# Four input tiles transposed by DMA on SyncE's queue instead of by TensorE, and the loads around them in a new order

## The chip, the cores and the metric

The kernel runs on one core of a Trainium2 chip. The metric is device time in microseconds. A core has TensorE (PE: matmuls and transposes into PSUM; PEld is its weight load, which runs beside it), VectorE (DVE), ScalarE (ACT), GpSimd (POOL) and SyncE (SP). SP, ACT and POOL each issue DMA transfers, which all share 16 DMA engines. Each engine executes its own instructions in order and waits on semaphores for the others.

## The reference

The input x has 2048 rows of 640 features. Rows are normalised; the result feeds a dilated sliding-window attention (32 heads of 20, window of 8 positions, 2 apart) and a gated product, and both are added to x.

```python
xn = _layernorm(x)                          # (2048, 640)
# attention
q, k, v = split(xn @ wqkv)                  # 32 heads of 20
idx = pos[:, None] - 2 * arange(8)          # 8 earlier positions, 2 apart
logits = einsum("bhsd,bhswd->bhsw", q, k[idx]) * Dh ** -0.5   # masked to -1e9 where idx < 0
o = einsum("bhsw,bhswd->bhsd", softmax(logits), v[idx])
A = o.reshape(B, S, D) @ wo
# gated product, 1536 wide
Bout = ((xn @ w_gate) * (xn @ w_up)) @ w_down
return x + A + Bout
```

All inputs, weights and the output are bfloat16.

## The kernel before

The 2048 rows are 16 tiles of 128 rows, and 4 chunks of 4 tiles. Nothing is issued as it is written in the source: every step is added to a plan (`add`) with an engine, a cost in us, what it depends on, and for transfers a size (`kb`) or a time before which they are not thought to land (`floor`). `Plan.order` then walks the engines like a list scheduler, each time taking the step with the least slack, and the program is emitted in that order. So costs, floors and dependences decide the order of instructions on every engine, in the whole kernel.

For each tile t, `ln(t)` makes the statistics on VectorE (`ln_stats` L251, twice; `ln_aggr` L257 and L259), GpSimd the reciprocal root (`ln_rstd` L265), VectorE again the normalised tile, in place (`ln_apply` L270). Tiles of x come from a pool of 5 buffers. `transposes(t)` then puts the tile, transposed, into `xnT` of its chunk (2 buffers):

- tiles 0 to 3: two groups of TensorE transposes (L345), each copied out of PSUM at L351;
- tiles 4 to 7 (t under `XDMA`, 8): five TensorE transposes of 128x128 (L331) into one PSUM tile, and one ScalarE copy (L335);
- tiles 8 to 15: one DMA transpose on SP's queue (L339).

At its end `transposes(t)` loads tile t+5 (L166): tiles 5 to 7 on SP, tiles 8 to 12 on ACT's queue, 13 to 15 on POOL's.

Per chunk, TensorE computes q and k (`qk`, L403, copied out by ScalarE at L410) and v (`vproj`, L436, copied out at L442 and stored to a scratch `vD` in device memory by POOL, L457). `prodlog` makes, for each of the 8 window positions, the elementwise product of q with the shifted k (VectorE, L474, 1.4 us each), and after four of them TensorE sums over the head's features into the logits (`lg`, L484, 20 matmuls). A few values are masked (L496, first chunk only), ScalarE copies the logits out (L497), and a DMA transpose on SP (L505, "LT") puts rows on partitions. `softmax` (L519 to L541) needs both LT transposes of the chunk. `load_v8(t)` reads the 8 shifted values of tile t back from `vD` (1280 KB, SP, L551, 3 buffers); `av` multiplies them with the weights and sums (L571, L580, L584, L586), and the result goes through a DMA transpose (L593, "oT").

`glu` is 12 pairs of matmul groups (L610) with wg and wu, copied out by ScalarE (L615) and multiplied on VectorE into hT (L626). `down` adds the products with wd (L648) and wo (L651) in one PSUM tile, VectorE adds x (L657), and the result is stored (L679). PSUM has 6 rotating banks ("ps") for all groups but the logits, which have two of their own ("pl").

Transfers on SP are issued in program order. The ones the change touches are, before: x0 to x3, wq, x4, wk, x5 to x7, wg, wu, the values of tile 0, wd, the first LT transpose, the values of tile 1, the second LT transpose, wo in four pieces (L231), the values of tile 2, the third LT transpose (chunk 1).

Of the kernel before, what the change touches and what calls it, by code (L numbers as in the profile page):

```python
# [9 lines left out]
ACT = mybir.ActivationFunctionType  # L10
# [21 lines left out]
class Plan:  # L32
# [8 lines left out]
    def add(self, eng, cost, fn, deps=(), occ=None, after=(), kb=0):  # L41
        s = Step(eng, cost, fn, deps, occ, after)
        s.kb = kb
        s.idx = len(self.steps)
        self.steps.append(s)
        return s
# [51 lines left out]
def kernel(  # L98
# [11 lines left out]
    nc = tc.nc  # L110
# [15 lines left out]
    CH = 4  # L126
# [36 lines left out]
    def load_x(t, eng=None):  # L163
        def fn():
            x = new(("x", t), [P, D], BF, "x", 5)
            (eng or nc.sync).dma_start(out=x[:], in_=x_flat[t * P : (t + 1) * P, :])  # L166
        return fn
# [3 lines left out]
    def wload(dst, src, eng=None):  # L171
        return lambda: (eng or nc.sync).dma_start(out=dst[:], in_=src.rearrange("(i p) f -> p i f", p=P))
# [9 lines left out]
    def load(at, fn, deps=()):  # L182
        s = chain[0] = add("SP", 2.0, fn, deps, occ=0.45, after=[chain[0]])
        s.floor = at
        return s
# [110 lines left out]
        XT[t] = inline("DVE", 0.443, ln_apply(t), [RS[t]], 0.4)  # L296

    def ln(t):
        turn = [XT.get(t - (2 if t < CH else 1)), GL.get(t - 1)] if t <= CH else []
        a = add("DVE", 0.48, ln_stats(t, 0), [X[t], GL.get(t - 3), *turn], occ=0.395)  # L300
        a = add("DVE", 0.48, ln_stats(t, 1), [a], occ=0.395)
        a = GL[t] = add("DVE", 0.39, ln_aggr(t), [a], occ=0.3)
        b = RS[t] = add("POOL", 0.56, ln_rstd(t), [a])
        XT[t] = add("DVE", 0.443, ln_apply(t), [b], occ=0.35)
# [10 lines left out]
        main = add("PE", cost + 0.165, fn, [main, *waits, *deps], occ=cost)  # L315
        return main

    XDMA = 8
    GP = {}

    def transposes(t):
        c, q = divmod(t, CH)

        def slot():
            if q == 0:
                new(("xnT", c), [P, KT, CS], BF, "xnT", 2)

        def pe():
            ps = new(("pst", t), [P, KT, P], BF, "ps", 6, psum)
            for g in range(KT):  # L330
                nc.tensor.transpose(ps[:, g, :], T["x", t][:, g * P : (g + 1) * P], ident[:])  # L331

        def ev():
            slot()
            nc.scalar.copy(T["xnT", c][:, :, q * P : (q + 1) * P], T["pst", t][:])  # L335

        def dma():
            slot()
            nc.sync.dma_start_transpose(out=T["xnT", c][:, :, q * P : (q + 1) * P], in_=T["x", t][:])  # L339

        def half(g0, g1, n):
            def pe():
                ps = new(("pst", t, n), [P, KT, P], BF, "ps", 6, psum)
                for g in range(g0, g1):
                    nc.tensor.transpose(ps[:, g, :], T["x", t][:, g * P : (g + 1) * P], ident[:])  # L345

            def ev():
                if n == 0:
                    slot()
                o, i = T["xnT", c][:, g0:g1, q * P : (q + 1) * P], T["pst", t, n][:, g0:g1, :]  # L350
                nc.scalar.copy(o, i) if t or n == 0 else nc.vector.tensor_copy(o, i)  # L351
            return pe, ev

        if t < CH:
            pa, ea = half(0, 3, 0)
            pb, eb = half(3, KT, 1)
            a = pe_main(0.17, pa, [XT.get((t, 0), XT[t])])
            TX[t] = add("ACT", 0.5, ea, [a], occ=0.42)
            ring.append(TX[t])
            a = pe_main(0.11, pb, [XT[t]])  # L360
            if t:
                TT[t] = add("ACT", 0.42, eb, [a, TX[t]], occ=0.33)
                behind(VE[t - 1][0], TT[t])
            else:
                TT[t] = inline("DVE", 0.4, eb, [a], 0.33)
            ring.append(TT[t])
        elif t < XDMA:
            a = pe_main(0.28, pe, [XT[t]])
            TT[t] = add("ACT", 0.695, ev, [a], occ=0.6)
            ring.append(TT[t])  # L370
        else:
            a = TT[t] = add("SP", 2.8, dma, [XT[t], GP.get(c - 2)], occ=1.28, kb=200)
        if t + 5 < W:
            X[t + 5] = load(11.9 + 0.45 * t, load_x(t + 5), [a])
        elif t + 5 < NT:
            e, dge = ("ACT", nc.scalar) if t < XDMA else ("POOL", nc.gpsimd)
            X[t + 5] = add(e, 6.0, load_x(t + 5, dge), [a], occ=0.45, kb=0 if t < XDMA else 160)

    Q, Kk, LASTPW = {}, {}, {}
    HALOCP = {}  # L380
# [85 lines left out]
    def prodlog(c):  # L466
        for g in range(2):
            n = 2 * c + g
            for j in range(4):
                i = 4 * g + j  # L470

                def mul(i=i):
                    p = new(("pw", c, i), [P, KT, CS], BF, "pw", 5)
                    nc.vector.tensor_tensor(p[:], T["q", c][:], T["k", c][:, :, DIL * i : DIL * i + CS], ALU.mult)  # L474

                m = 8 * c + i
                PW[m] = add("DVE", 1.48, mul, [*Q[c], *Kk[c], LL.get((m - 5) // 4) if m >= 5 else None], occ=1.395)
            LASTPW[c] = PW[m]

            def lg(g=g):  # L480
                l = new(("lps", c, g), [P, 512], F32, "pl", 2, psum)
                for i in range(KT):
                    for j in range(4):
                        nc.tensor.matmul(l[H * j : H * (j + 1), :], lhsT=Ek[:, i, :], rhs=T["pw", c, 4 * g + j][:, i, :],  # L484
                                         start=(i == 0), stop=(i == KT - 1), tile_position=(0, H * j),
                                         skip_group_check=True)

            LL[n] = add("PE", 1.28, lg, [*[PW[8 * c + 4 * g + j] for j in range(4)], LE.get(n - 2), CE], occ=1.195)
            LL[n].urgent = True
            LL[n].margin = 1.0  # L490

            def ev(g=g):
                L = new(("L", c, g), [P, CS], BF, "L", 2)
                if c == 0:
                    ps = T["lps", c, g]
                    nc.vector.tensor_tensor(ps[:, 0:HALO], ps[:, 0:HALO], negm[:, g, :], ALU.add)  # L496
                nc.scalar.copy(L[:], T["lps", c, g][:])  # L497

            LE[n] = add("ACT", 0.585, ev, [LL[n], SS.get(n - 2), CM], occ=0.5)

            def tr(g=g):
                if g == 0:
                    new(("LT", c), [P, CH, W, H], BF, "LT", 1)
                out = T["LT", c][:].rearrange("p t (g w) h -> p t g (w h)", g=2)[:, :, g, :]
                nc.sync.dma_start_transpose(out=out, in_=T["L", c, g][:])  # L505

            early = [SPLAST[0]] if c == 0 else []
            SS[n] = SPLAST[0] = add("SP", 3.5, tr, [LE[n], DD.get(2 * c - 1), DD.get(2 * c - 2)], occ=1.25, after=early, kb=160)
            if c == 0 and g == 0:
                load_v8(1)  # L510
                SPLAST[0] = V8[1]

    def softmax(c, hf):
        n = 2 * c + hf
# [30 lines left out]
    def load_v8(t):  # L545
        def fn():
            v = new(("v8", t), [P, W, D], BF, "v8", 3)
            r0 = t * P
            src = vD[r0 : r0 + P, :]
            src = bass.AP(tensor=src.tensor, offset=src.offset, ap=[[D, P], [DIL * D, W], [1, D]])  # L550
            nc.sync.dma_start(out=v[:], in_=src)  # L551
        order = [SPLAST[0]] if t < CH - 1 else [SS[2 * (t // CH) + 1]] if t % CH in (1, 2) else []
        V8[t] = add("SP", 6.0, fn, [VS[t], VS.get(t - 1), O16.get(t - 3), CZ], occ=0.5, after=order, kb=1280)
        if t < 3:
            SPLAST[0] = V8[t]
            V8[t].floor = (30.5, 0, 0)[t]

    def load_down():
        WL["d"] = SPLAST[0] = add("SP", 8, wload(wd, B_w_down), after=[SPLAST[0]], occ=0.5, kb=1920)

    def load_out():
        WL["o"] = SPLAST[0] = add("SP", 8, wo_load, after=[SPLAST[0]], occ=2.7, kb=1100)
# [154 lines left out]
    vproj(2, (1,))  # L717
    CE = add("POOL", 1.2, consts_e, [C0, RS[3]])
    CM = add("POOL", 1.1, consts_m, [CE])
    WL["g"] = load(17.2, wload(wg, B_w_gate))  # L720
    WL["u"] = load(23.2, wload(wu, B_w_up))
    qk(0, 0, CS, (0,))
    for t in (4, 5):
        ln(t)
        transposes(t)
    qk(0, 0, CS, (1,))
    for t in (6, 7):
        ln(t)
        transposes(t)
    vproj(3)  # L730

    def between(c, work):
# [6 lines left out]
    def attention(c):  # L739
        if c == 0:  # L740
            SPLAST[0] = WL["u"]
            load_v8(0)
            load_down()
        prodlog(c)
        if c == 0:
            load_out()
            load_v8(2)
        for hf in range(2):
            softmax(c, hf)
        for q in range(CH):  # L750
            av(c * CH + q)
# [47 lines left out]
```

## Time and profile before

| | us |
|---|---|
| median of 3 runs | 267.35 (267.27 to 267.51) |
| the profiled execution | 267.32 |
| its span, first to last instruction | 265.6 |
| ScalarE busy in the span | 108.2 |
| GpSimd busy in the span | 40.7 |
| one value load (L551), median from issue to landing | 7.0 |
| one DMA transpose of a tile of x (L339), median from issue to landing | 4.3 |

Busy time of an engine says how much of the span it was executing. The chain of waits follows the instruction that ended last back through what released it, step by step; what lies on it sets the time. The timeline gives instructions in order, with the idle time in front of each and what ended it. For a transfer, the row on SPq, ACTq or POOLq is the time its engine spent on issuing, and "to landing" runs from there to the arrival of the data.

### The profile page before, as it was taken

How to read it: one execution, taken by the hardware profiler on the slowest of the kernel's cores; microseconds unless marked ns; L12 is line 12 of the kernel's file. 1: busy time of each engine (PE TensorE's matmuls, PEld its weight loads, DVE VectorE, ACT ScalarE, POOL GpSimd, SP SyncE). 2: the span in 40 equal slices, each digit the busy share in tenths (PEclk: the TensorE clock that was granted, in tenths of full speed). 3: DMA queues.
4: the chain of work that ended last, by engine and by line, in shares of the span. 5: the costliest groups of instructions: out<-in, count | busy, mean ns of one | idle time of the engine just before them, and what ended most of it. 6: DMA issues, size and time to landing. Idle time of an engine off the chain costs nothing.

```text
span 265.6 us, 4131 instructions
## 1 busy us (share of the span) xinstructions
PE 260.1 (98%) x1594; PEld 141.5 (53%) x1594; DVE 215.5 (81%) x338; ACT 108.2 (41%) x200; POOL 40.7 (15%) x84
## 2 busy tenths in 40 slices
PE   7999999999999999999999999999999999999994
PEld 2645455444577546444466754644447764445772
DVE  5784999999999999999992999999829999921221
ACT  2666564655400166555510135555552005554000
POOL 4641025200021311400000100420000113000000
PEclk9999999999999999999999999999999999999999
DMA  7999998957496391993136937594129279110001
GB/s 224 375 406 390 368 205 263 295 137 222 113 239 144 74 367 59 299 307 32 25 71 97 334 136 222 144 288 41 20 71 346 67 230 151 25 25 0 27 33 41
DMA packets 47875, 45.89 MB, mean 173 GB/s; under 512 B 21954, under 2 KB 45008, under 8 KB 47856
## 3 DMA queue, kind: packets, MB, share of 16 engines
q1 hardware_dynamic: 43440, 35.95, 48.4%
q0 software_dynamic: 2384, 8.05, 9.7%
q10 hardware_dynamic: 2032, 1.64, 1.9%
q8 instruction: 12, 0.20, 0.4%
q14 instruction: 7, 0.06, 0.1%
HBM read 35.39 MB, written 5.26 MB: 153 GB/s over the span
## 4 chain that ended last, share of the span: by engine, by line
PE 95%; DVE 2%; DMA 1%; issue 0%
PE ps L610 39%; PE ps L648 20%; PE ps L403 16%; PE ps L651 8%; PE ps L436 7%; PE pl L484 4%; DVE st L251 1%; DMA x<-in_A_x_dram 1%; PE ps L345 0%; PE ps L331 0%; DVE x L270 0%; DVE xr L657 0%; DVE mv L257 0%; DVE ve L259 0%; DVE xnT L351 0%
## 5 line engine op out<-in xcount | busy, mean ns | idle before, releaser
L610 PE MATMUL ps<-xnT,wg 128*128 128x512 bf16 x240 | 59.7, 380 | 0.0
L610 PE MATMUL ps<-xnT,wu 128*128 128x512 bf16 x240 | 59.7, 380 | 0.0
L648 PE MATMUL ps<-wd,hT 128*128 128x320 bf16 x384 | 57.4, 300 | 0.0
L474 DVE TENSOR_TENSOR pw<-q,k 128x2560 bf16<-128x2560 bf16 x32 | 46.4, 1486 | 3.2 <-ACT k L410 3.0
L648 PEld LDWEIGHTS <-hT 128*128 128x128 bf16 x384 | 37.4, 98 | 15.9 <-issue 0.8
L571 DVE TENSOR_TENSOR v<-v,a 128x5120 bf16<-128x5120 bf16 x16 | 45.1, 2818 | 0.1
L615 ACT CAST gs<-ps 128x512 bf16<-128x512 f32 x48 | 28.1, 585 | 40.2 <-PE ps L610 40.2
L610 PEld LDWEIGHTS <-wu 128*128 128x128 bf16 x240 | 23.3, 98 | 28.7 <-issue 0.8
L610 PEld LDWEIGHTS <-wg 128*128 128x128 bf16 x240 | 23.3, 98 | 28.1 <-issue 0.8
L615 ACT CAST us<-ps 128x512 bf16<-128x512 f32 x48 | 28.1, 585 | 23.3 <-PE ps L610 22.3
L626 DVE TENSOR_TENSOR hT<-gs,us 128x512 bf16<-128x512 bf16 x48 | 19.8, 420 | 14.4 <-ACT us L615 14.3
L657 DVE TENSOR_TENSOR xr<-ps,xr 128x320 bf16<-128x320 f32 x32 | 14.8, 486 | 19.4 <-PE ps L651 15.6
L651 PE MATMUL ps<-wo,oT 128*128 128x320 bf16 x160 | 27.0, 299 | 0.0
L679 POOL DMA_DIRECT2D out_dram<-xr x14 | 7.6, 546 | 122.7 <-DVE xr L657 122.7
L580 DVE TENSOR_TENSOR v<-v 128x2560 bf16<-128x2560 bf16 x16 | 23.8, 1485 | 0.1
L436 PE MATMUL ps<-wv,xnT 128*128 128x320 bf16 x160 | 23.2, 300 | 0.4 <-ACT xnT L351 0.4
L403 PE MATMUL ps<-xnT,wk 128*128 128x512 bf16 x100 | 22.4, 380 | 0.0
L403 PE MATMUL ps<-xnT,wq 128*128 128x512 bf16 x100 | 22.2, 379 | 0.0
L436 PEld LDWEIGHTS <-xnT 128*128 128x128 bf16 x160 | 15.2, 98 | 7.2 <-ACT xnT L351 0.5
L651 PEld LDWEIGHTS <-oT 128*128 128x128 bf16 x160 | 15.6, 98 | 6.1
L410 ACT CAST q<-ps 128x512 bf16<-128x512 f32 x20 | 11.7, 585 | 16.7 <-PE ps L403 16.7
L497 ACT CAST L<-pl 128x512 bf16<-128x512 f32 x8 | 4.7, 585 | 29.2 <-PE pl L484 26.4
(58 smaller groups left out, 193.1 us busy)
## 6 DMA issues: line engine op xcount, KB each, us to landing
v<-vD SPq DMA_DIRECT2D x16, 1280.0 KB, 7.0
vD<-v_t POOLq DMA_DIRECT2D x16, 160.0 KB, 4.6
xr<-in_A_x_dram POOLq DMA_DIRECT2D x16, 160.0 KB, 5.9
out_dram<-xr POOLq DMA_DIRECT2D x14, 160.0 KB, 2.2
wg<-in_B_w_gate_dram SPq DMA_DIRECT2D x1, 1920.0 KB, 11.2
wu<-in_B_w_up_dram SPq DMA_DIRECT2D x1, 1920.0 KB, 16.5
wd<-in_B_w_down_dram SPq DMA_DIRECT2D x1, 1920.0 KB, 22.0
x<-in_A_x_dram SPq DMA_DIRECT2D x8, 160.0 KB, 4.5
```

The costliest lines, as they stand in the source:

```text
L403: nc.tensor.matmul(T[key][:, 0:n], lhsT=(wk if r else wq)[:, i, j * P : (j + 1) * P], rhs=T["xnT", c][:, i, lo : lo + n], start=(i == 0), ...
L410: nc.scalar.copy(dst, T[key][:, 0:n])
L436: nc.tensor.matmul(T["psv", t, n][:, 0:NS], lhsT=T["xnT", c][:, i, q * P : (q + 1) * P], rhs=wv[:, i, n * NS : (n + 1) * NS], start=(i == ...
L474: nc.vector.tensor_tensor(p[:], T["q", c][:], T["k", c][:, :, DIL * i : DIL * i + CS], ALU.mult)
L571: nc.vector.tensor_tensor(v[:].rearrange("p w (j h) -> p w j h", j=Dh, h=H), v[:].rearrange("p w (j h) -> p w j h", j=Dh, h=H), T["a", n][ ...
L580: nc.vector.tensor_tensor(v[:, 0:4, :], v[:, 0:4, :], v[:, 4:8, :], ALU.add)
L610: nc.tensor.matmul(ps[:], lhsT=(wu if r else wg)[:, i, f * P : (f + 1) * P], rhs=T["xnT", c][:, i, :], start=(i == 0), stop=(i == KT - 1))
L615: nc.scalar.copy(s[:], T[key][:])
L626: nc.vector.tensor_tensor(h[:], T["gs", c, f][:], T["us", c, f][:], ALU.mult)
L648: nc.tensor.matmul(ps[:, 0:NS], lhsT=T["hT", c, f][:, q * P : (q + 1) * P], rhs=wd[:, f, sl], start=(f == 0), stop=(f == FT - 1 and not wo ...
L651: nc.tensor.matmul(ps[:, 0:NS], lhsT=T["oT", t][:, g, :], rhs=wo[:, g, sl], start=False, stop=(g == KT - 1 and f1 == FT))
L657: nc.vector.tensor_tensor(T["xr", t][:, sl], T["psD", t, n][:, 0:NS], T["xr", t][:, sl], ALU.add)
```

## The change

Tiles 4 to 7 take the third path of `transposes`, a DMA transpose on SP each. They join the chain of SP's loads (`chain[0]`), so that they are issued after x5 to x7 and before wg. Behind wg come the loads of tiles 9 to 12, which were on ACT's queue, then wu. The values of tile 0 move behind the first LT transpose, the values of tile 1 and wd behind the second, and wo and the values of tile 2 follow. The order within `ln` for tiles 5 to 7 gets explicit dependences on the tiles before them. Floors and costs in the plan differ, and with them the order that the plan gives to every later step.

```diff
 def ln(t):
-    turn = [XT.get(t - (2 if t < CH else 1)), GL.get(t - 1)] if t <= CH else []
+    turn = [XT.get(t - (1 if t == CH else 2)), GL.get(t - 1)] if t < 2 * CH else []
...
-XDMA = 8
+XDMA = 4
...
-        a = TT[t] = add("SP", 2.8, dma, [XT[t], GP.get(c - 2)], occ=1.28, kb=200)
+        if c == 1:
+            a = TT[t] = chain[0] = add("SP", 3.0, dma, [XT[t]], occ=1.28, after=[chain[0]])
+        else:
+            a = TT[t] = add("SP", 2.8, dma, [XT[t], GP.get(c - 2)], occ=1.28, kb=200)
     if t + 5 < W:
         X[t + 5] = load(11.9 + 0.45 * t, load_x(t + 5), [a])
-    elif t + 5 < NT:
-        e, dge = ("ACT", nc.scalar) if t < XDMA else ("POOL", nc.gpsimd)
-        X[t + 5] = add(e, 6.0, load_x(t + 5, dge), [a], occ=0.45, kb=0 if t < XDMA else 160)
+    elif t == 3:
+        X[t + 5] = add("ACT", 6.0, load_x(t + 5, nc.scalar), [a], occ=0.45)
+    elif 8 <= t < NT - 5:
+        X[t + 5] = add("POOL", 6.0, load_x(t + 5, nc.gpsimd), [a], occ=0.45, kb=160)
...
             if c == 0 and g == 0:
-                load_v8(1)
-                SPLAST[0] = V8[1]
+                load_v8(0)
+                SPLAST[0] = V8[0]
...
-        V8[t].floor = (30.5, 0, 0)[t]
+        V8[t].floor = (42.5, 0, 0)[t]
...
-WL["g"] = load(17.2, wload(wg, B_w_gate))
-WL["u"] = load(23.2, wload(wu, B_w_up))
-qk(0, 0, CS, (0,))
-for t in (4, 5):
+for t in range(CH, 2 * CH):
     ln(t)
     transposes(t)
-qk(0, 0, CS, (1,))
-for t in (6, 7):
-    ln(t)
-    transposes(t)
+WL["g"] = load(28.5, wload(wg, B_w_gate))
+for t in range(9, 13):
+    X[t] = load(30.0, load_x(t), [TT[t - 5]])
+WL["u"] = load(36.0, wload(wu, B_w_up))
+qk(0, 0, CS)
 vproj(3)
...
     if c == 0:
         SPLAST[0] = WL["u"]
-        load_v8(0)
-        load_down()
     prodlog(c)
     if c == 0:
+        load_v8(1)
+        load_down()
         load_out()
         load_v8(2)
```

The program that results has, on SP: x0 to x3, wq, x4, wk, x5 to x7, four transposes of tiles 4 to 7, wg, x9 to x12, wu, the first LT transpose, the values of tile 0, the second LT transpose, the values of tile 1, wd, wo, the values of tile 2; the third LT transpose is now behind the transposes of tiles 8 to 11. On TensorE the 20 transposes at L331 are gone; the order of the rest is the same up to the first group with wg, after which six of the eight logits groups (L484) stand at other places among the matmuls. VectorE has the same instructions in another order.

## The prediction, made before the changed kernel ran

> **What bounds the kernel now.** First the page's busy times, TensorE's granted clock and the chain of waits.
>
> ```profile
> PE 260.1 (98%) x1594; PEld 141.5 (53%) x1594; DVE 215.5 (81%) x338; ACT 108.2 (41%) x200; POOL 40.7 (15%) x84
> PEclk9999999999999999999999999999999999999999
> PE 95%; DVE 2%; DMA 1%; issue 0%
> ```
>
> TensorE is the bound, at full clock. Next the chain in order of time (start, length, what), where the changed work lies:
>
> ```profile
> 12.04 5.40 PE ps L403 x25
> 17.44 0.56 PE ps L331 x10
> 17.99 5.40 PE ps L403 x25
> 23.39 0.56 PE ps L331 x10
> 23.95 1.36 PE ps L436 x10
> 25.30 6.58 PE ps L403 x30
> ```
>
> From 12 us on the pieces touch, so whatever is taken off TensorE shortens the kernel one for one, as long as nothing comes late. The rest is therefore a search for lateness, in the timeline (start, length, engine, instruction) and the times to landing:
>
> ```profile
> 24.04 7.10 DVE L474 TENSOR_TENSOR pw<-q,k 128x2560 bf16<-128x2560 bf16 x5 [3.02 <-ACT k L410]
> 42.24 1.20 SPq L505 DMA_TRANSPOSE LT<-L  x1
> 45.71 0.28 DVE L519 TENSOR_TENSOR m<-LT 128x256 bf16<-128x256 bf16 x1
> 86.58 0.49 DVE L657 TENSOR_TENSOR xr<-ps,xr 128x320 bf16<-128x320 f32 x1
> 87.53 0.77 PEld L484 LDWEIGHTS <-Ek 128*32 128x32 bf16 x20 [0.26 <-issue]
> 135.48 5.19 SPq L339 DMA_TRANSPOSE xnT<-x  x4
> ```
>
> VectorE starts its products when k is out (24.04), its softmax at 45.71, and at 87 us it is less than a microsecond ahead of TensorE's logits (products end 86.68, use 87.53). That thin lead is the thing to watch. Four tile transposes take SP 5.19 us of issue, 1.30 each.
>
> **Removed: TensorE's 20 transposes.** On the chain 17.99 - 17.44 = 0.55 and 23.95 - 23.39 = 0.56: 1.11 us. Their four ScalarE copies (L335, two of 1.29 us for two tiles, 2.58 in all) are off the chain, with ScalarE 41% busy: nothing.
>
> **Added: four DMA transposes.** VectorE gets x5 at 12.65 as before. Statistics cost 0.8, aggregation 0.35 to 0.4, an apply 0.35, GpSimd's root 0.55 in between; in the new order applies end near 13.9, 16.0, 17.1 and 18.5. So the last transpose issues at 18.6. GpSimd's 1.26 us of mask fills now stand ahead of tile 5's root, but it is free by 14.4, when that root is due. Landing: 2.6 us in the quiet row at 135.5, 5.3 at 71.5 behind a value load, 8.3 for the third LT transpose at 49.3, the worst of its kind. wk lands at 5.12 + 7.1 = 12.2 and x7 near 13.6, and wg is now behind, so the queue is quiet and I take 2.6: landed 21.2. TensorE needs it for the second q at 25.30 - 1.11 = 24.19. Spare 3.0 us; 0.3 at 5.3; 2.7 late at 8.3.
>
> The skill weighs against this: "VectorE: DVE Perf Modes", section "The three transpose paths", gives 390 ns for a 128x128 block on TensorE, 1309 by DMA, and its rules prefer TensorE. By that, twenty blocks in a row would be an estimated 26 us and land near 40, some 16 us late. This trace has five blocks landing in 2.6 us and costing TensorE 0.28, so the row decides.
>
> **Moved: wg, x9 to x12, wu.** wg goes from 10.13 to about 19.9. Rate: 407 GB/s in the windows from 14 to 22 us. wg is 1.97 MB, 4.8 us, so 26.0; four tiles 1.6, so 27.7; wu 32.5. VectorE wants x9 at 24.04 - 0.55 + 7.02 = 30.5, TensorE wg at 44.24 - 1.11 = 43.1 and wu 1.1 later: nothing, hidden by 2.8 and 11 us or more. SP is then free for the first LT transpose at 33.1 (before: 34.24). ACT's queue loses four loads, which cost only 0.35 us of issue each.
>
> **Moved: the values of tile 0 behind that transpose.** Issued 34.4, landing 5.9 (row at 60.7) to 8.4 (row at 35.6): 40.3 to 42.8; their product starts near 53 before and, by the lead below, at 50.1. Nothing. The second LT transpose is behind them on the queue. It issues at 42.24 less 1.1 or a little more, and before it landed in 3.1 us behind just such a load: 44.2. Bounds 2.4 (the row at 89.5) to 8.3: 43.5 to 49.4.
>
> **VectorE's lead, new order.** From the first product to the softmax took 45.71 - 24.04 = 21.67 before with twelve products; now eleven (a product is 1.40): 23.49 + 20.27 = 43.76. So the softmax waits for the LT transpose until 44.2. Call that m. From m on I add the timeline's steps: statistics of the softmax 2.95, normalisation 2.23, hT 0.33, value product 2.74, its sums 1.40 and 1.26. The third value product comes at m + 21.25 = 65.5, the last hT of the chunk at m + 27.65 = 71.9, the last output row block at m + 33.15, then three L657 (0.40) and a product: m + 35.75 = 80.0. TensorE: the third logits group (1.19) has left the gated product, so the down stage starts at 71.44 - 1.11 - 1.19 = 69.1; it needs the last hT 30 matmuls of 0.136 later, 73.2 (spare 1.3); and the logits group now comes after 85 matmuls, at 80.7 (spare 0.7, as thin as the 0.85 before). The values of tile 1, wanted at m + 12, are first behind the LT transpose: in time.
>
> **Moved: wd, wo, values of tile 2 into one convoy.** Behind the LT transpose SP now has values 1.31, wd 1.97, wo 0.82, values 1.31 MB, beside POOL's stores and reloads of 1.32: 6.7 MB. Such loads ran at 363 to 382 GB/s in the windows from 24 to 34 us; slowest mean is the 274 of the windows from 42 to 56. From 43.8 that is 18.4 us, 62.2, or 24.5 us, 68.3; I take the first, since the slow windows had only wo's small pieces queued and here wd is in front. Wanted 65.5: spare 3.3, or 2.8 late. wd itself is in by about 53, wanted 69.1. The output transposes and values of tile 3 follow on a queue that is free by then: they are wanted at 70.5 and 71.9.
>
> **Later chunks.** Carrying the same additions on, VectorE reaches the second softmax at 93 (92.99 before) with TensorE 1.1 earlier; the remaining logits groups have their products 2 us or more ahead, and the hT of the second chunk start 0.6 us earlier than before. Tiles 8 to 11 transpose from 69.1, wanted at 90. Nothing. The tail (262.01 to 265.6) is the same.
>
> **Sum.** 265.6 - 1.11 = 264.49 span. Around the span lie 267.32 - 265.6 = 1.72: 266.21. The profiled run is 0.03 under the median shown, so 266.2 serves for both, 0.4% faster. A measurement here can tell about 0.2%, 0.53 us: faster is under 266.8, slower above 267.9.
>
> **Rivals.**
> 1. *The lead is eaten.* The second LT transpose lands 1.2 to 2.4 late (4.3 to 5.5 us, like the 4.4 of the first LT transpose at 34.2 behind bulk loads). Then TensorE waits at the third logits group for lateness less 0.7: 0.5 to 1.7, and the time is 266.7 to 267.9, about 267.3. For it: the lead, and a value load just in front in the same queue. Against: the 3.1 was measured behind one too. At the far bound, 8.3, the wait is 4.5 and the time 270.7. 17%.
> 2. *The convoy makes it slower.* The values of tile 2 land late, VectorE stands before the third product, and its lateness past 0.7 goes to TensorE at the same logits group. It is slower than before once the values are over 0.7 + 1.11 = 1.8 late, a mean rate under 6.7/(67.3 - 43.8) = 0.285 MB/us. At 274 it is 2.8 late: TensorE waits 2.1, 268.3; with wo's pieces at the 215 GB/s of the windows from 44 to 46 (0.8 us more) it waits 2.9, 269.1. For it: six loads in one queue that were spread from 16 to 57 us. Against: full queues ran at 363. 13%.
> 3. *The transposes of x come late.* At 8.3 to landing TensorE waits 2.7 before the second q: 268.9. It pays nothing up to 5.6 and turns into a loss over 6.7. Against: no bulk load is in front of them now. 4%.
>
> That the change does not do what it says is excluded by the program: TensorE's stream is 20 transposes shorter. Forecast 66%: 266.2, with 265.9 to 266.6 its own range. Chances: faster 0.68 (the forecast and a little of the first rival), same 0.17 (most of the first, the milder half of the second and third), slower 0.15. The range goes from 265.9 to 267.7, which leaves out the heavier part of the second rival.
>
> **What would show it.** Right: no L331; q and k of chunk 0 end at 22.8 and the second q starts at 24.2 without a wait on a DMA; the fourth tile transpose issues by 19 and lands by 22; the softmax starts at 43.8 to 44.5; L484 of the third group at 80.7 without idle time in front. Wrong: idle TensorE ahead of L403 at 24 us or ahead of L484 at 81, VectorE waiting for v<-vD near 65, or a wait in the down stage for hT or oT.

## The result, and the profile after

| | before | after |
|---|---|---|
| median, us | 267.35 (267.27 to 267.51, 5 runs) | 266.25 (266.05 to 266.96, 5 runs) |
| ratio, 95% interval | | 0.9960 [0.9950, 0.9971] |
| profiled execution, us | 267.32 | 266.25 |
| its span, us | 265.6 | 264.5 |

The kernel is 0.4% faster: 1.1 us, twice the 0.53 that a measurement here can tell from nothing. First the page of the kernel after: busy time by engine, TensorE's granted clock, and the chain's shares. Line numbers from L403 on are four higher than before (L403 is L407, L484 is L488, L648 is L652).

```profile
PE 258.5 (98%) x1556; PEld 140.8 (53%) x1574; DVE 215.5 (81%) x338; ACT 106.5 (40%) x196; POOL 40.7 (15%) x84
PEclk9999999999999999999999999999999999999999
PE 97%; DVE 1%; issue 0%
```

TensorE is still the bound at full clock. Its count falls by 38, not by 20: some matmul records are missing from this trace, so counts are not used below, only times. The chain of waits of the kernel after, in order of time (start, length, what):

```profile
12.28 0.21 PE ps L407
12.49 0.05 issue
12.55 10.52 PE ps L407 x48
23.07 1.36 PE ps L440 x10
24.43 0.21 PE ps L407
24.64 0.05 issue
24.70 6.21 PE ps L407 x28
30.90 1.19 PE pl L488 x20
...
80.02 0.68 PE ps L655 x5
80.70 1.38 PE pl L488 x20
82.08 1.74 PE ps L652 x12
...
261.21 0.49 DVE xr L661
```

The two pieces of L331 are gone. q and k are one run from 12.28 to 23.07, and the second q follows the v group with no gap, so the transposes by DMA are in time. One piece is longer than it was: the third logits group takes 1.38 us where every other takes 1.19. That is a wait of 0.19. From the start of q to the last VectorE addition the chain takes 261.21 - 12.28 = 248.93, against 262.01 - 12.04 = 249.97 before: 1.04 less. Measuring from q's start leaves out that q begins at 12.0 to 12.4 in one execution or another, of any of these kernels.

SP's timeline of the kernel after (start, length of issue):

```profile
14.57 6.54 SPq L339 DMA_TRANSPOSE xnT<-x  x4
21.17 0.57 SPq L172 DMA_DIRECT2D wg<-in_B_w_gate_dram  x1
...
33.13 1.20 SPq L509 DMA_TRANSPOSE LT<-L  x1
...
40.88 1.19 SPq L509 DMA_TRANSPOSE LT<-L  x1
...
43.50 8.31 SPq L231 DMA_DIRECT2D wo<-in_A_wo_dram  x4
51.91 0.68 SPq L555 DMA_DIRECT2D v<-vD  x1
```

The four transposes take 6.54 us of issue, not four times 1.3: the first alone takes 2.57. The value load of tile 2 can be issued only at 51.91, because one of wo's four pieces in front of it holds SP for 6.24 us. VectorE's timeline of the kernel after shows how near that came to being too late:

```profile
23.73 7.10 DVE L478 TENSOR_TENSOR pw<-q,k 128x2560 bf16<-128x2560 bf16 x5 [2.40 <-ACT k L414]
...
41.42 0.45 DVE L270 TENSOR_SCALAR x<-x,mv,rstd 128x640 bf16<-128x640 bf16 x1 [0.74 <-POOL rstd L265]
...
44.58 0.28 DVE L523 TENSOR_TENSOR m<-LT 128x256 bf16<-128x256 bf16 x1
...
65.93 2.82 DVE L575 TENSOR_TENSOR v<-v,a 128x5120 bf16<-128x5120 bf16 x1
...
72.12 0.42 DVE L630 TENSOR_TENSOR hT<-gs,us 128x512 bf16<-128x512 bf16 x1
...
79.30 1.48 DVE L478 TENSOR_TENSOR pw<-q,k 128x2560 bf16<-128x2560 bf16 x1
```

The values of tile 2 land 14.0 us after issue, at 65.9, and their product starts at 65.93 with no idle time in front: just in time. The fourth product for the third logits group, in the last line, ends at 79.30 + 1.48 = 80.78, and TensorE was free for it at 80.70: that is the wait.

### The profile page after: what moved, and what is told of

It is laid out like the page before. It is cut to its first block, busy times and chain, and to the rows that moved or that the text cites. A ratio compares the mean times of both kernels' runs of the same rounds, so it can differ in the third digit from the quotient of the medians.

```text
span 264.5 us, 4077 instructions
## 1 busy us (share of the span) xinstructions
PE 258.5 (98%) x1556; PEld 140.8 (53%) x1574; DVE 215.5 (81%) x338; ACT 106.5 (40%) x196; POOL 40.7 (15%) x84
## 4 chain that ended last, share of the span: by engine, by line
PE 97%; DVE 1%; issue 0%
PE ps L614 39%; PE ps L652 20%; PE ps L407 16%; PE ps L655 8%; PE ps L440 7%; PE pl L488 4%; PE ps L242 2%; DVE st L251 1%; PE ps L345 1%; DVE x L270 0%; DVE xr L661 0%; DVE xnT L351 0%; DVE gs L201 0%; DVE mv L257 0%; DVE ve L259 0%
## 5 line engine op out<-in xcount | busy, mean ns | idle before, releaser
L614 PE MATMUL ps<-xnT,wg 128*128 128x512 bf16 x227 | 59.0, 379 | 0.7
L614 PE MATMUL ps<-xnT,wu 128*128 128x512 bf16 x240 | 59.6, 379 | 0.0
L652 PE MATMUL ps<-wd,hT 128*128 128x320 bf16 x384 | 57.4, 299 | 0.0
L652 PEld LDWEIGHTS <-hT 128*128 128x128 bf16 x384 | 37.3, 98 | 16.3 <-issue 1.3
L407 PE MATMUL ps<-xnT,wk 128*128 128x512 bf16 x99 | 22.4, 379 | 0.1
L407 PE MATMUL ps<-xnT,wq 128*128 128x512 bf16 x96 | 22.0, 379 | 0.2
```

What stands on the lines that cost most here:

```text
L407: nc.tensor.matmul(T[key][:, 0:n], lhsT=(wk if r else wq)[:, i, j * P : (j + 1) * P], rhs=T["xnT", c][:, i, lo : lo + n], start=(i == 0), ...
L614: nc.tensor.matmul(ps[:], lhsT=(wu if r else wg)[:, i, f * P : (f + 1) * P], rhs=T["xnT", c][:, i, :], start=(i == 0), stop=(i == KT - 1))
L652: nc.tensor.matmul(ps[:, 0:NS], lhsT=T["hT", c, f][:, q * P : (q + 1) * P], rhs=wd[:, f, sl], start=(f == 0), stop=(f == FT - 1 and not wo ...
```

## The experiments

All diffs are against the kernel after. Each result is the median of its runs, with the ratio to the kernel before, which ran on the same chip.

**The moved loads alone.** The theory says that the gain is TensorE's 20 transposes and nothing else; a rival says that the new order of loads helps or hurts by itself. So tiles 4 to 7 go back to TensorE, the loads keep their new order.

```diff
-        elif t < XDMA:
+        elif t < 2 * CH:
...
-    for t in range(CH, 2 * CH):
+    WL["g"] = load(28.5, wload(wg, B_w_gate))
+    qk(0, 0, CS, (0,))
+    for t in (4, 5):
+        ln(t)
+        transposes(t)
+    qk(0, 0, CS, (1,))
+    for t in (6, 7):
         ln(t)
         transposes(t)
-    WL["g"] = load(28.5, wload(wg, B_w_gate))
...
-    qk(0, 0, CS)
```

> Tiles 4 to 7 are transposed by TensorE again; wg, x9 to x12, wu, the values of tiles 0 to 2, wd and wo keep the order of the changed kernel. TensorE's order is that of the kernel before, 20 transposes included. Theory (the gain is the 1.11 us of transposes taken off TensorE, the moved loads give nothing of themselves): no gain, 267.35 within 0.3. Rival (the new order of the loads gives the gain, by bringing VectorE's inputs earlier): 266.3.

267.36 us (267.29 to 267.78), ratio 1.0001 [0.9992, 1.0009]. In its chain of waits both pieces of transposes are back:

```profile
17.46 0.56 PE ps L331 x10
...
23.42 0.56 PE ps L331 x10
23.97 1.36 PE ps L440 x10
```

So the new order of loads is worth nothing by itself, neither way. The whole gain hangs on the transposes.

**Two tiles instead of four.** If the gain is TensorE's time, half the transposes must give half of it.

```diff
-        elif t < XDMA:
+        elif t in (6, 7):
...
-    for t in range(CH, 2 * CH):
+    for t in (4, 5):
         ln(t)
         transposes(t)
...
+    qk(0, 0, CS)
+    for t in (6, 7):
+        ln(t)
+        transposes(t)
...
-    qk(0, 0, CS)
```

> Only tiles 4 and 5 go through the DMA transpose, 6 and 7 stay on TensorE; loads as in the changed kernel, TensorE's order that of the kernel before less 10 transposes. Theory (0.28 us of TensorE per tile): half the gain, 266.8 within 0.25. Rival (the gain comes from where the logits groups stand in the new order): 267.35.

266.63 us (266.59 to 266.68), ratio 0.9972 [0.9962, 0.9982]. The chain from q to the last addition takes 261.51 - 12.10 = 249.41: 0.56 less than before, one group of ten transposes. The gain scales, and it comes with TensorE's order of before, so the new places of the logits groups are not what gives it.

**The transposes alone.** The other half of the change: the transposes stay on DMA, the loads behind them go back (x9 to x12 on ACT's queue, values of tile 0 and wd behind wu).

```diff
-        elif t == 3:
+        elif t < 8:
...
-        elif 8 <= t < NT - 5:
+        elif t < NT - 5:
...
-                load_v8(0)
-                SPLAST[0] = V8[0]
+                load_v8(1)
+                SPLAST[0] = V8[1]
...
-    for t in range(9, 13):
-        X[t] = load(30.0, load_x(t), [TT[t - 5]])
...
+            load_v8(0)
+            load_down()
         prodlog(c)
         if c == 0:
-            load_v8(1)
-            load_down()
```

> The four DMA transposes stand in front of wg, but x9 to x12 stay on ACT's queue and the values of tile 0 and wd stay right behind wu, as before. Theory (the moves are what keeps the transposes free): behind the fourth transpose, which landed at 23.4, lie 7.2 MB on SP and 0.7 on ACT, 20 us at 390 GB/s, so the first LT transpose lands at about 44 instead of 36.4 and the second at about 50 instead of 44.1; the softmax is 5 us late and TensorE waits 3 to 5 us for hT or the logits' products: 269 to 271. Rival (the transposes alone do it, the moves are no part of it): 266.2 to 266.4.

273.55 us (272.66 to 275.53), ratio 1.0251 [1.0221, 1.0281]: slower, and by more than expected. TensorE's waits from 20 to 110 us (what waits for what: us in total, times, longest):

```profile
PE ps L652 <- DVE hT L630: 2.7, 1, 2.7
PE ps L655 <- DMA oT<-o: 1.3, 1, 1.3
PE pl L488 <- DVE pw L478: 1.3, 1, 1.3
```

The two LT transposes of chunk 0 take 10.9 and 9.8 us to landing here, behind a load of wd that itself takes 20.9; in the kernel after they take 3.3 and 3.2. Their data are in at 33.98 + 10.9 = 44.9 and 40.97 + 9.8 = 50.8, 8.5 and 6.7 later than after. The test is not clean: the plan also put five more products of the next chunk in front of the softmax, which starts at 56.37 instead of 44.58, 5.6 us after the second LT is in. And the 2.7 us wait cost more than 2.7. The 16 matmuls behind it took 3.68 us (from 80.13 to the start of the next group at 83.81) instead of 2.17. These windows show why (us; busy time of PE, PEld, DVE, ACT and POOL, then granted clock, DMA share and GB/s):

```profile
78.00:80.00 2.00, 0.00 (x0) 0.00 (x0) 2.00 (x3) 0.00 (x0) 0.44 (x1) 0.93 0.88 182
80.00:82.00 2.00, 1.87 (x7) 0.99 (x8) 1.97 (x4) 0.00 (x0) 0.00 (x0) 0.50 0.95 205
82.00:84.00 2.00, 2.00 (x12) 1.27 (x11) 1.97 (x3) 0.00 (x0) 0.54 (x1) 0.71 0.97 295
84.00:86.00 2.00, 2.00 (x17) 1.43 (x16) 1.97 (x2) 0.00 (x0) 0.00 (x0) 1.00 1.01 311
```

The granted clock fell to half. So the transposes gain nothing with the old order of loads: there wd (in at 23.41 + 20.9 = 44.3) and the values of tile 0 (21.46 + 17.1 = 38.6), pushed back with wg and wu by the transposes, are still under way when the first LT is issued. How much of the loss comes from the late LT, and how much from the plan's other order of products, this run does not separate.

**Transposes behind wg and wu.** The prediction set the landing of the fourth transpose against TensorE's second q. Here the bulk goes first.

```diff
+    WL["g"] = load(17.2, wload(wg, B_w_gate))
+    WL["u"] = load(23.2, wload(wu, B_w_up))
     for t in range(CH, 2 * CH):
         ln(t)
         transposes(t)
-    WL["g"] = load(28.5, wload(wg, B_w_gate))
...
-    WL["u"] = load(36.0, wload(wu, B_w_up))
...
-            SPLAST[0] = WL["u"]
+            SPLAST[0] = chain[0]
```

> The changed kernel with wg and wu in front of the four transposes on SP's queue instead of behind; TensorE's order is that of the changed kernel. Theory (a transpose lands behind the loads in front of it in its queue): wu landed at 27.1 in the kernel before, so the fourth transpose lands at 28 to 31 and TensorE waits 4 to 6 us before the second q: 270 to 272. Rival (a transpose is not held up by loads in front of it, or TensorE has other cover): 266.2 to 266.6.

273.96 us (273.71 to 274.48), ratio 1.0249 [1.0236, 1.0263]. The transposes take 3.4, 6.7 and up to 12.7 us to landing. The one wait on them (view of the waits), and then windows with the same columns as above:

```profile
PE ps L407 <- DMA xnT<-x: 5.0, 1, 5.0
```

```profile
26.00:28.00 2.00, 0.00 (x0) 0.00 (x0) 2.00 (x3) 0.00 (x0) 0.00 (x0) 0.95 1.20 295
28.00:30.00 2.00, 0.59 (x1) 0.28 (x3) 2.00 (x2) 0.00 (x0) 0.00 (x0) 0.50 0.99 228
30.00:32.00 2.00, 1.92 (x5) 0.73 (x5) 2.00 (x5) 0.40 (x1) 0.00 (x0) 0.50 0.47 147
32.00:34.00 2.00, 2.00 (x6) 0.66 (x5) 0.25 (x1) 0.45 (x2) 0.00 (x0) 0.50 0.00 0
34.00:36.00 2.00, 2.00 (x9) 0.81 (x8) 0.00 (x0) 0.91 (x2) 0.00 (x0) 0.84 0.00 0
36.00:38.00 2.00, 2.00 (x11) 0.94 (x10) 0.00 (x0) 1.09 (x2) 0.00 (x0) 1.00 0.00 0
```

Of 7.7 us over the kernel after (273.96 - 266.25) the wait is 5.0. The second q and the k behind it then run from 29.27 to 38.54, 9.27 us, where the kernel after needs 24.43 to 30.90, 6.47: 2.8 us more, at a granted clock of 0.50 for most of it. 5.0 + 2.8 = 7.8. So the place in front of wg is needed, and here a late transpose cost TensorE over half as much again as it was late.

**The convoy, relieved and loaded.** Two runs on the values of tile 2. In the first they stand in front of wd and wo.

```diff
             load_v8(1)
+            load_v8(2)
             load_down()
             load_out()
-            load_v8(2)
```

> The changed kernel with the values of tile 2 in front of wd and wo on SP's queue. Theory (they land just in time, nothing stands still for them, and the 0.2 us of waiting at the third logits group comes from VectorE's sum, not from the load): they land near 54 instead of 65.9 and the time stays that of the changed kernel, 266.25 within 0.2. Rival (the convoy costs a little in some executions, which would be the spread from 266.05 to 266.96): 266.0 and a narrow spread.

266.15 us (266.00 to 266.24), ratio 0.9951 [0.9938, 0.9963]. The values are in by 42.73 + 12.3 = 55, some 11 us earlier, and nothing moves; its third logits group in the chain:

```profile
80.64 1.38 PE pl L488 x20
```

The same 0.19 of wait: the convoy costs the changed kernel nothing. In the second run the values of tile 1 are also copied once to a scratch in device memory, so that the queue has 1.31 MB more in front of wd, wo and the values of tile 2.

```diff
+            if t == 1:
+                extra = dram.tile([P, W, D], BF, name="extra")
+                nc.sync.dma_start(out=extra[:], in_=src)
```

> The changed kernel with one transfer more: the values of tile 1 are also copied to a scratch in device memory (1.31 MB, SP's queue), between the values of tile 1 and wd; nothing waits for it. In the changed kernel the values of tile 2 landed at 65.9 and their product started at 65.93. Theory (VectorE has no lead left at the third logits group, so lateness of the values goes through to TensorE one for one): 1.31 MB at 365 GB/s is 3.6 us, TensorE waits about 3.6 us more, 269.9; more if a copy inside device memory is slower. Rival (there are spare microseconds behind the third product, as my sum had it, 0.7, and elsewhere in the down stage): 266.3 to 268.

269.11 us (268.94 to 269.15), ratio 1.0061 [1.0048, 1.0075]: slower than before. The chain of waits has left TensorE and runs through the queue:

```profile
55.52 13.26 DMA v<-vD
68.81 2.83 DVE v L578
```

The product starts at 68.81 instead of 65.93, 2.9 later, and the time is 269.11 - 266.14 = 2.97 over that of the unchanged kernel in the same series. One for one: the 65.9 of the kernel after is the edge, with no spare behind it. TensorE did not stand at the logits group alone: 1.57 us of its waiting lies at an hT of the down stage, which VectorE makes behind the late product.

**The third logits group, later.** The 0.19 us is a wait for a product, at a place which the plan chose. A margin in the plan, for this group alone, makes the plan put it 17 matmuls later; the fourth group moves back too, by 9. (The best of the series.)

```diff
-            LL[n].margin = 1.0
+            LL[n].margin = 1.8 if n == 2 else 1.0
```

> The changed kernel with the planner's margin behind the third logits group raised from 1.0 to 1.8, which puts that group 17 matmuls later in TensorE's order and the later ones by similar amounts. Theory (at the third logits group VectorE has no lead and TensorE waits 0.2 us, more in some executions): 266.0 to 266.1, with a spread of 0.2 or less. Rival (the 0.2 is the cost of the place, not a wait): 266.25 as it was.

265.89 us (265.81 to 265.91), ratio 0.9942 [0.9928, 0.9955]. In its chain of waits the group is back to 1.19:

```profile
82.78 1.19 PE pl L488 x20
...
260.80 0.49 DVE xr L661
```

260.80 - 12.05 = 248.75, that is 0.18 less than after: the wait. The median is 0.25 under that of the unchanged kernel in the same series (266.14). That is less than the 0.53, but the runs of the two do not overlap (265.81 to 265.91 and 266.09 to 266.24), and the chain agrees.

**The unchanged kernel once more.** One of the five runs of the result, 266.96, lay 0.7 above the others; the kernel ran again beside the last ones.

> The changed kernel once more, for the spread of its times beside the other three. Theory (no lead at the third logits group, so small delays of transfers show): 266.2 to 266.3 with single runs up to 0.7 above the lowest. Rival (the one high run of five was an accident): all within 0.3 of each other.

266.14 us (266.09 to 266.24, 5 runs), ratio 0.9952 [0.9940, 0.9965]. The chain takes 261.11 - 12.19 = 248.92, as in the first profile, and the 266.96 did not come back.

**Why the first tile transpose is slow.** Two runs on one point behind the misjudged landing. In the first, a small transpose (128x128) goes to SP near its start.

```diff
+    def load_x3():
+        load_x(3)()
+        nc.sync.dma_start_transpose(out=Ek[:].rearrange("p a b -> p (a b)")[:, 0:P], in_=ident[:])
...
-    X[3] = load(5.3, load_x(3))
+    X[3] = load(5.3, load_x3, [C0])
```

> Open: why the first of the four moved tile transposes takes 2.57 us of issue and 4.4 us to landing where its three successors take 1.22 to 1.24 and 2.6 to 3.5. Here one small transpose by DMA (128x128) stands on SP's queue near its start, in front of wq. Theory (the first transpose by DMA in a program pays something once): the small one takes that, the first tile transpose issues in 1.2 to 1.3 us and lands in 2.6 to 3.0, the fourth lands at 21.5 to 22.2 instead of 23.4, TensorE's chain is as before, 266.2 to 266.6. Rival (it is what else runs at 14 us, the load of x8 and the stores of the values): the first still takes 2.2 to 2.6 to issue and 3.7 to 4.6 to land, same time.

266.28 us (266.04 to 266.45), ratio 0.9961 [0.9941, 0.9981]. The first tile transpose issues in 2.06 us and lands in 4.0.

In the second, x8 is loaded behind wg too.

```diff
-        elif t == 3:
-            X[t + 5] = add("ACT", 6.0, load_x(t + 5, nc.scalar), [a], occ=0.45)
...
-    for t in range(9, 13):
+    for t in range(8, 13):
```

> The same question from the other side: the load of x8 leaves ACT's queue and stands behind wg with x9 to x12, so that it doesn't run beside the first tile transpose. Theory (first of its kind): nothing changes there, the first still issues in 2.2 to 2.6 us and lands in 3.7 to 4.6. Rival (the load of x8 holds it up): 1.2 to 1.3 and 2.6 to 3.0, the fourth lands at 21.5 to 22.2. Either way x8 is in by 28 to 29, where VectorE needs it at about 28 to 30, so the time is 266.2 and up to 0.5 more if x8 is late.

266.28 us (265.83 to 266.37), ratio 0.9951 [0.9929, 0.9974]. Here it is 1.95 and 4.0. Neither reason explains it alone: without it, 1.2 to 1.3 and 2.6 to 3.0 were expected. One profile of each says no more, for the issue is no fixed cost: over the profiles in which nothing near it was edited, the longest issue of the four is 2.57 (after), 2.20 (the same kernel again), 1.37 (values of tile 2 first) and 1.29 us (third logits group later). What sets it stays open; it costs nothing here. A by-product: the plan puts the third logits group 17 matmuls later in this kernel as well, and its chain, 260.77 - 12.03 = 248.74, is the one without the wait. That the wait is a matter of place is thus seen twice in the chain; the medians of these two kernels, 266.28 both, do not show it.

## Why the prediction was right, point by point

- **TensorE's 20 transposes, 1.11 us.** Right, and all of the gain: nothing with the transposes on TensorE, half with two tiles. The chain adds up like this: 1.12 us of L331 off; the second q and first k group, 30 matmuls, 6.47 instead of 6.58, so another 0.11 off; 0.19 of new wait on. 1.12 + 0.11 - 0.19 = 1.04, as measured. The 0.11 was priced at nothing, as ScalarE's copies "off the chain". Both kernels that keep the copy for tiles 6 and 7 on ScalarE show it (25.33 to 31.92, 6.59, and 24.81 to 31.39, 6.58), and in the profile before the copy ends at 25.20, 0.1 ahead of the group's start. That it is this copy fits, but was not tried by itself.
- **The fourth transpose, landed 21.2, spare 3.0.** In time, but mis-sized: issued at 19.9, landed at 23.4, spare 1.0. Of the issue's 1.3 us, 0.5 comes from tile 7's apply, which ended at 19.0 instead of 18.5 (VectorE got x5 at 13.31, not at 12.65), and the rest from the first transpose's issue of 2.57, behind which the others queue; 0.9 comes from a landing of 3.5 instead of 2.6.
- **wg 26.0, wu 32.5.** Mis-sized and hidden. wg was issued at 21.17, 1.3 later than told, and the sum let it move at 407 GB/s from its issue; in the window from 22 to 24 us the engines moved 132 GB/s, and 415 only from 24 on. wg was in at 29.0 and wu at 36.0; wg was wanted at 43.25.
- **The second LT transpose, 44.2.** Right: 40.88 + 3.2 = 44.1. The softmax began at 44.58 instead, since VectorE started its products 0.24 later (23.73) and stood 0.74 for GpSimd's root in front of an apply at 41.42. The first rival's late LT did not come, though its place was right: the wait is at the third logits group.
- **The convoy, landed 62.2, wanted 65.5.** The worst size: 65.9, between the two bounds (62.2 and 68.3). Taking the faster rate for wo's pieces was the wrong choice: wo's issue took 8.31 us where it had taken 2.67, and the last load waited behind it. The DMA engines were busy all the while (share 1.0 or more in every window of 2 us from 46 to 66), so what was lost is rate: 224 GB/s from 56 to 60, where wo's first two pieces landed (58.8 and 59.6). With the softmax at 44.58 the product was due at 44.58 + 21.25 = 65.83, so the spare was 0, not 3.3. The second rival's mechanism is real: 2.9 us later cost 2.97. Its price of lateness less 0.7 was too low, because that 0.7 was gone.
- **The lead at the third logits group, 0.7.** Really -0.19. Of the 0.9 between them, 0.4 is the later softmax (44.58 for 44.2) and the rest the sum of steps behind it: the product was to end at 44.58 + 35.75 = 80.33 and ended at 80.78. The down stage started at 69.15 (69.1 predicted), and the last hT ended at 72.5, wanted 73.2, in time as told.
- **The third rival** needed a bulk load in front. With one, its price would have been too low as well: it counted the wait alone, and the clock falls with it.
- **The time.** 266.2 against 266.25. By luck the two mis-sized terms on the chain, 0.11 and 0.19, nearly cancel, and so do two outside it: q began 0.24 later (12.28), and the tail, from the last addition to the end of the span, which was held to be the same, went from 265.6 - 262.01 = 3.59 to 264.5 - 261.21 = 3.29. What moved these two is not known. The large ones, 2.2 us at the transposes and 3.7 in the convoy, ended within the spare the sum had given them, in the convoy with nothing left.

## What to carry to other kernels

Work taken off the engine that bounds pays one for one only if the queue that takes it over is cleared for it: here the same four transposes gave 1.1 us with the loads rearranged and lost 6 with them in the old order (the plan's other order of products included). Size the small pieces of a convoy by the slowest stretch seen with such pieces, and ask which issue holds up the queue, not only how many bytes stand in it. When the list of waits shows none, compare equal groups on the chain with each other: 1.38 among 1.19 was the only trace of a wait, and moving one group by 17 matmuls took it away.

## What the runs showed of the hardware that was not expected

- **A long wait of TensorE can be charged twice.** After 5.0 us of idling the granted clock was 0.50 from 28 to 34 us, and the next 30 matmuls took 2.8 us more. After 2.7 us of idling it fell as well and cost 1.5 us. In the run with the extra transfer a wait of 1.6 us left it at 1.00 in the windows that follow. The Trainium skill, "TensorE: Matmul & The Clock Gate", in its part on the HAM clock gate, puts the fall to half rate at an idle window of about 3.4 us; the runs agree on the half, but here 2.7 us was enough. The half clock does not last as long as the wait: in windows of 0.2 us it runs from 79.7 to 83.1 in the one run and from 27.8 to 34.6 in the other, 3.4 and twice 3.4 us, and it begins 2.3 and 3.5 us into the idling. What was lost is about half of the time that TensorE worked in it: from 80.13 to 83.1, 3.0 us, and from 29.27 to 34.6, 5.4.
- **The loads behind the transposes were slow to start, and not because these were still under way.** wg is issued at 21.17, the last transpose lands at 23.4; these are windows of the kernel after (columns as above):

```profile
20.00:22.00 2.00, 2.00 (x11) 0.88 (x9) 0.63 (x3) 1.04 (x2) 0.55 (x1) 1.00 0.73 146
22.00:24.00 2.00, 2.00 (x14) 1.18 (x13) 0.27 (x1) 1.45 (x4) 0.00 (x0) 1.00 0.61 132
24.00:26.00 2.00, 1.95 (x12) 0.98 (x11) 2.00 (x2) 1.18 (x3) 0.58 (x1) 1.00 1.03 415
```

It looks as if the loads wait for the transposes, but two other runs say no. With the third logits group later wg is issued at 20.11 and the last transpose is in at 18.8 + 2.6 = 21.4; with the transposes alone, 20.21 and 18.94 + 4.46 = 23.4. Two windows of the first and two of the second:

```profile
22.00:22.40 0.40, 0.40 (x3) 0.20 (x2) 0.00 (x0) 0.39 (x1) 0.00 (x0) 1.00 0.14 38
22.80:23.20 0.40, 0.40 (x5) 0.29 (x3) 0.00 (x0) 0.32 (x1) 0.00 (x0) 1.00 1.03 392
```

```profile
22.40:22.80 0.40, 0.40 (x4) 0.20 (x2) 0.00 (x0) 0.00 (x0) 0.00 (x0) 1.00 0.34 100
22.80:23.20 0.40, 0.40 (x5) 0.29 (x3) 0.00 (x0) 0.00 (x0) 0.00 (x0) 1.00 0.84 328
```

In the first the engines are slow still when the last transpose is in, in the second they are fast before it is. In all three runs they pass 300 GB/s 2.4 to 2.7 us after the issue of wg (in the kernel after at 23.6). What takes these 2.4 us is open.

- **A DMA issue can hold up SP.** One of wo's four pieces took 6.24 us to issue behind 3.3 MB of other loads, where all four took 2.67 before.
